# Attention loads and writes in half-size pieces, at most two under way: a linear-attention and expert kernel on one core

## The chip, the cores and the metric

The kernel runs on one core of one Trainium2 chip. The metric is device time in microseconds (us), as the median of several runs; a profiled execution of the same kernel gives the span and the trace that the views below are taken from. Engines are named as in the profile: PE (TensorE matmuls), PEld (TensorE weight loads), DVE (VectorE), ACT (ScalarE), POOL (GpSimd), SP (SyncE, whose queue issues the transfers that this document is about).

## What is computed

Linear attention without a softmax, an RMS norm, and then a layer of eight experts with balanced assignment. All data are float32.

```
kv  = einsum('bhsd,bhse->bhde', k, v)          # B=8, H=8, S=576, D=64
out = einsum('bhsd,bhde->bhse', q, kv)
x   = out / sqrt(mean(out^2) + 1e-6) * g_norm  # then (B*S, H*D) = (4608, 512)
logits = x @ w_gate                            # 8 experts, 576 tokens each
# greedy: all (token, expert) pairs in falling order of logit; a token takes
# the expert if it has none yet and the expert has room
out[tokens of e] = relu(x[tokens of e] @ w1[e]) @ w2[e]     # 512 -> 1024 -> 512
```

## The kernel before

The program has three stages, one after the other: attention, the assignment of tokens to the first expert, and the experts (with the next expert's assignment beside the matmuls of the present one). The change lies in the attention stage alone.

**Attention.** The loop runs over the eight batches b. `load(name, b)` brings one of k, v, q of a batch into a tile of 128 partitions x 4 head pairs (`NP`) x 9 rows (`R`) x 64, that is 1152 KB, by one transfer from SP (L75). Each of the three names has two buffers, so batch b + 2 takes the buffer of batch b. The first six loads (batches 0 and 1) are issued at the start. `prepare(b)` is a generator of four steps: it multiplies k by v into `kv_ps` (L273, 144 matmuls in two halves, head pairs 0 and 1 and then 2 and 3), adds the halves on ACT and DVE (`odd` L278, `kv` L280), copies the result to `kvx` on POOL (L286), calls for k and v of b + 2, transposes q into `qt` (L301), computes the gate's weights seen through kv (L312, L320), and last calls for q of b + 2. `work(b)` makes the output tiles of batch b: `tiles()` runs, for each of 3 to 5 token tiles, 32 small matmuls (`o_ps`, L349), a square and a copy on ACT (`sq` L355, `o_sb` L356), a reduction on DVE (`ms` L357); then the norm's factor, the logits `lg` (L371), and a copy of the factor into `o_sb` on POOL (L374). While batch b is worked on, the steps of `prepare(b + 1)` are laid between its tiles.

**Writes.** Each `o_sb` (4 or 5 token tiles of 128 x 576 numbers, 288 KB each; batch 7 makes two, of 3 and 2 token tiles) goes to `x_dram` by one transfer from SP (L375). The transfers are put on a list, `writes`, and issued in order at the end of a batch while the list holds `LAG = 5` or more; after batch 7 all are issued. `o_sb` has `LAG + 1 = 6` buffers, so batch 6 writes into batch 0's buffer and must find its write landed.

**Order.** In this stage PE, DVE, ACT and SP are under `manual_schedule`: their instructions run in the order in which the program makes them. So the queue of SP holds, in this order, the loads k0 v0 q0 k1 v1 q1 k2 v2 q2 ... q7, then nine writes, then the loads of the first expert's weights. Four small transfers (`g_col`, `gw`) are issued from ACT at the start.

**Assignment and experts.** `control(0)` finds thresholds by seven rounds of comparison on DVE (L242) and small matmuls (L440), then POOL gathers the rows of `x_dram` (L575); `layers(t)` runs the two matmuls of each expert (L639, L650).

The lines that tie the loads to the work are these:

```
    def prepare(b):                     # ... after the matmuls of kv(b)
        if b + 2 < B:
            load("k", b + 2)
            load("v", b + 2)
...                                     # ... after the transposes of q(b)
        if b + 2 < B:
            load("q", b + 2)
```

## Time and profile before

| | |
|---|---|
| median of 3 runs | 753.87 us (753.83 to 755.69) |
| profiled execution, its own time | 750.37 us |
| span in the trace | 748.4 us |
| PE busy | 640.3 us (86%) |
| attention stage, up to the last logits `lg` (L371) | 0 to 135.4 us |
| first assignment, up to the first row gather (L575) | 135.5 to 172.3 us |
| experts | 172.3 us to the end |
| PE idle in the attention stage put down to "issue", between 14 and 127 us | 25.3 us |
| loads of k, v and q | 24 of 1152 KB |
| writes of x_dram | 9: four of 1152 KB, three of 1440 KB, one of 864 KB, one of 576 KB |

The profiled execution is 3.50 us below the median of the runs; 1.97 us of its own time lie outside its span. "Issue" is idle time of an engine for which the trace shows no semaphore that it waited for. In the transfer views, "to landing" is the time from the issue on SP to the last of the transfer's completion counts.

### The profile page before, as it was taken

How to read it: one execution, taken by the hardware profiler on the slowest of the kernel's cores; microseconds unless marked ns; L12 is line 12 of the kernel's file. 1: busy time of each engine (PE TensorE's matmuls, PEld its weight loads, DVE VectorE, ACT ScalarE, POOL GpSimd, SP SyncE). 2: the span in 40 equal slices, each digit the busy share in tenths (PEclk: the TensorE clock that was granted, in tenths of full speed). 3: DMA queues.
4: the chain of work that ended last, by engine and by line, in shares of the span. 5: the costliest groups of instructions: out<-in, count | busy, mean ns of one | idle time of the engine just before them, and what ended most of it. 6: DMA issues, size and time to landing. Idle time of an engine off the chain costs nothing.

```text
span 748.4 us, 12187 instructions
## 1 busy us (share of the span) xinstructions
PE 640.3 (86%) x5001; PEld 405.7 (54%) x5001; DVE 352.9 (47%) x1253; ACT 161.6 (22%) x331; POOL 93.0 (12%) x113
## 2 busy tenths in 40 slices
PE   2787756113999999999999999999999999999994
PEld 2676645002764576457546744774476457547741
DVE  3455646785556365555645554656365642010000
ACT  0466446001110211021112112110211021122100
POOL 0101000002002300310031004001400322010011
PEclk9999998555999999999999999999999999999998
DMA  8988694108004500720090017004500638010001
GB/s 306 363 275 312 222 392 155 75 1 295 1 1 165 195 1 0 261 98 1 15 323 22 1 62 291 8 0 145 207 8 1 230 129 296 14 43 7 1 28 35
DMA packets 40838, 93.32 MB, mean 125 GB/s; under 512 B 2896, under 2 KB 2896, under 8 KB 40784
## 3 DMA queue, kind: packets, MB, share of 16 engines
q1 hardware_dynamic: 34192, 72.49, 27.2%
q0 software_dynamic: 5888, 20.06, 7.5%
q8 instruction: 39, 0.64, 0.3%
q10 hardware_dynamic: 704, 0.02, 0.1%
q14 instruction: 15, 0.12, 0.1%
HBM read 72.50 MB, written 20.05 MB: 124 GB/s over the span
## 4 chain that ended last, share of the span: by engine, by line
issue 62%; PE 17%; POOL 10%; DVE 7%; DMA 2%; ACT 1%; ACTq 0%; POOLq 0%; DVEq 0%
POOL out_dram L621 5%; POOL xg L575 5%; PE h_ps L639 5%; PE o_ps L349 3%; PE kv_ps L273 2%; PE qt_ps L301 2%; PE y_ps L650 2%; DMA gw<-in_moe_w_gate_dram 1%; DVE over L242 1%; DMA xg<-x_dram,ids 1%; PE n_ps L440 1%; ACT sq L355 1%; DVE ms L357 1%; DVE need L446 0%; PE w_ps L320 0%
## 5 line engine op out<-in xcount | busy, mean ns | idle before, releaser
L639 PE MATMUL h_ps<-xt,w_sb 128*128 128x288 f32 x1024 | 270.7, 415 | 0.0
L650 PE MATMUL y_ps<-w_sb,hid 128*128 128x512 f32 x512 | 227.2, 597 | 0.0
L639 PEld LDWEIGHTS h_ps<-xt,w_sb 128*128 128x128 f32 x1024 | 188.7, 191 | 51.9 <-issue 5.7
L650 PEld LDWEIGHTS y_ps<-w_sb,hid 128*128 128x128 f32 x512 | 94.8, 190 | 105.2 <-issue 104.3
L642 ACT ACTIVATE hid<-h_ps 128x288 f32<-128x288 f32 x128 | 52.5, 410 | 219.8 <-PE h_ps L639 219.8
L621 POOL DMA_INDIRECT out_dram<-y_sb,outs x40 | 41.1, 1026 | 452.5 <-ACT y_sb L653 401.6
L612 DVE TENSOR_TENSOR xs<-xg 128x512 f32<-128x512 f32 (+1 forms) x40 | 27.1, 690 | 90.9 <-DMA xg<-x_dram,ids 45.8
L242 DVE TENSOR_TENSOR over<-mx,cand 128x1152 bf16<-128x1152 f32 (+3 forms) x52 | 67.5, 1298 | 1.6
L653 ACT COPY y_sb<-y_ps 128x512 f32<-128x512 f32 x32 | 18.7, 585 | 209.2 <-PE y_ps L650 209.2
L663 DVE TENSOR_TENSOR y_sb<-y_ps,y_part 64x512 f32<-64x512 f32 x8 | 5.5, 683 | 95.4 <-ACT y_part L662 95.4
L575 POOL DMA_INDIRECT xg<-x_dram,ids x40 | 38.9, 972 | 73.2 <-DVE up L582 36.9
L349 PE MATMUL o_ps<-kvx,qt 64*64 64x72 f32 x1152 | 34.5, 247 | 15.3 <-issue 13.2
L349 PEld LDWEIGHTS o_ps<-kvx,qt 64*64 64x64 f32 x1152 | 27.5, 148 | 20.7 <-issue 16.6
L440 PEld LDWEIGHTS <-over 128*128 128x128 bf16 x441 | 18.1, 97 | 38.1 <-DVE over L242 22.9
L616 PE MATMUL t_ps<-ident,xs 128*128 128x128 f32 (+1 forms) x160 | 23.9, 284 | 17.1 <-DVE xs L612 13.7
L461 DVE SCALAR_TENSOR_TENSOR at<-row_f,k_ps,cand 128x33 f32<-128x33 f32 x98 | 21.4, 257 | 34.3 <-PE k_ps L456 34.3
L273 PE MATMUL kv_ps<-v_sb,k_sb 64*64 64x64 f32 x1152 | 27.2, 243 | 11.1 <-issue 11.1
L440 PE MATMUL n_ps<-best,over 128*128 128x32 bf16 x441 | 19.2, 178 | 20.4 <-DVE cand L434 12.5
L617 ACT ACTIVATE xt<-t_ps,g_col 128x512 f32<-128x512 f32 (+1 forms) x40 | 24.4, 646 | 52.5 <-PE t_ps L616 52.4
L446 DVE TENSOR_TENSOR need<-goal,n_ps 32x8 f32<-32x8 f32 x49 | 7.5, 154 | 57.0 <-PE n_ps L440 57.0
L357 DVE TENSOR_REDUCE ms<-sq 128x8 f32<-128x512 f32 x36 | 24.3, 681 | 19.5 <-ACT sq L355 19.4
L616 PEld LDWEIGHTS t_ps<-ident,xs 128*128 128x128 f32 (+1 forms) x160 | 18.0, 149 | 26.6 <-issue 16.4
(162 smaller groups left out, 472.6 us busy)
## 6 DMA issues: line engine op xcount, KB each, us to landing
w_sb<-in_moe_w_dram SPq DMA_DIRECT2D x16, 1024.0 KB, 6.1
w_sb<-in_moe_w_dram SPq DMA_DIRECT2D x8, 2048.0 KB, 16.1
k_sb<-in_k_dram SPq DMA_DIRECT2D x8, 1152.0 KB, 6.6
v_sb<-in_v_dram SPq DMA_DIRECT2D x8, 1152.0 KB, 9.4
q_sb<-in_q_dram SPq DMA_DIRECT2D x8, 1152.0 KB, 7.4
x_dram<-o_sb SPq DMA_DIRECT2D x4, 1152.0 KB, 13.0
x_dram<-o_sb SPq DMA_DIRECT2D x3, 1440.0 KB, 13.9
x_dram<-o_sb SPq DMA_DIRECT2D x1, 864.0 KB, 3.7
```

The costliest lines, as they stand in the source:

```text
L242: nc.vector.tensor_tensor(over[:, c0:c1], mx[:, c0:c1].rearrange("p (c o) -> p c o", o=1).to_broadcast([P, c1 - c0, NCAND]), cand[:, 1:NCA ...
L273: nc.tensor.matmul(kv_ps[cs, l, r * D:(r + 1) * D], lhsT=k_sb[ls, r, j, :], rhs=v_sb[ls, r, j, :], start=(j < 2), stop=(j >= R - 2))
L349: nc.tensor.matmul(o_ps[n * HP:(n + 1) * HP, rp, (2 * r2 + l) * W:(2 * r2 + l + 1) * W], lhsT=turned_q[bn][ks, block // 2, l * HP:(l + 1) ...
L357: nc.vector.reduce_sum(out=ms[:, t * H:(t + 1) * H], in_=sq, axis=AXX)
L440: nc.tensor.matmul(n_ps, lhsT=over[:, c:c + G].rearrange("p c n -> p (c n)"), rhs=best[:, c:c + G].rearrange("p c e -> p (c e)"), start=(c ...
L575: nc.gpsimd.indirect_dma_start(out=xg[0:nr].rearrange("p h w -> p (h w)"), out_offset=None, in_=x_dram, in_offset=bass.IndirectOffsetOnAxi ...
L612: nc.vector.tensor_tensor(xs[0:nr].rearrange("p (h d) -> p h d", h=H), xg[0:nr, :, 0:D], xg[0:nr, :, D:D + 1].to_broadcast([nr, H, D]), op ...
L616: nc.tensor.transpose(t_ps[:, d, 0:nr], xs[0:nr, d * P:(d + 1) * P], ident[0:nr, 0:nr])
L621: put = nc.gpsimd.indirect_dma_start(out=out, out_offset=bass.IndirectOffsetOnAxis(ap=ids_of[t][0:nr, n:n + 1], axis=0), in_=y_sb[0:nr, :] ...
L639: nc.tensor.matmul(h_ps, lhsT=w1[:, 2 * (d % 2) + d // 2, f * P:(f + 1) * P], rhs=xt[:, d, cs], start=(d == 0), stop=(d == DC - 1))
L642: nc.scalar.activation(hid[:, f, cs], h_ps, ACT.Relu)
L650: nc.tensor.matmul(y_ps, lhsT=hid[:, f, a:a + nr], rhs=w2[:, f, :], start=(f == 0), stop=(f == FC - 1))
```

## The change

Each load becomes two transfers of two head pairs (576 KB). Each write becomes transfers of two token tiles (576 KB), with a last one of a single token tile (288 KB) where the count is odd. All of them go through `paced()`, which keeps a list of the transfers in order and gives each one a dependence on the transfer two places ahead of it: SP issues it only when that one has landed. The list of writes is emptied down to fewer than ten entries at the end of a batch instead of five. `o_sb` keeps its six buffers and the loads their two.

```diff
     loaded = {}
+    AHEAD = 2
+    issued = []
+
+    def paced(dma):
+
+        if len(issued) >= AHEAD:
+            tc.add_manual_dep(dma.ins, issued[-AHEAD].name,
+                              mybir.DependencyInfo(mybir.DependencyClass.Sync, mybir.DependencyReason.DATA),
+                              reason="paced loads")
+        issued.append(dma.ins)
 
     def load(name, b):
 
         src = {"k": k, "v": v, "q": q}[name]
         t = att.tile([P, NP, R, D], FT, name=f"{name}_sb", tag=name, bufs=2)
-        nc.sync.dma_start(
-            t.rearrange("p r j d -> p r (j d)"),
-            src[b].rearrange("h s d -> (h s) d").rearrange("(r p j) d -> p r (j d)", r=NP, j=R))
+        rows = src[b].rearrange("h s d -> (h s) d").rearrange("(r p j) d -> p r (j d)", r=NP, j=R)
+        for r in range(0, NP, NP // 2):
+            rs = slice(r, r + NP // 2)
+            paced(nc.sync.dma_start(t[:, rs].rearrange("p r j d -> p r (j d)"), rows[:, rs]))
         loaded[name, b] = t
...
-        writes.append(lambda: nc.sync.dma_start(
-            x_dram[c0 * P:(c0 + T) * P, :].rearrange("(t p) f -> p t f", p=P), o_sb.rearrange("p t h w -> p t (h w)")))
+        for x in range(0, T, 2):
+            y = min(x + 2, T)
+            writes.append(lambda x=x, y=y: paced(nc.sync.dma_start(
+                x_dram[(c0 + x) * P:(c0 + y) * P, :].rearrange("(t p) f -> p t f", p=P),
+                o_sb[:, x:y].rearrange("p t h w -> p t (h w)"))))
...
-            while len(writes) >= LAG or b + 1 == B and writes:
+            while len(writes) >= 2 * LAG or b + 1 == B and writes:
                 writes.pop(0)()
```

In the built program SP's queue holds 48 load pieces and 20 write pieces. Counting the pieces a, b and c of a transfer, its order at the end of the stage is ... q6a q6b W0a k7a k7b v7a v7b q7a q7b W0b W1a W1b W1c W2a ..., where W0 is batch 0's `o_sb`. The matmuls of kv wait for the pieces of k and v half by half (head pairs 0 and 1 for `a`, 2 and 3 for `b`); the first ACT copy into a reused `o_sb` waits for all pieces of that buffer's last write.

## The prediction

> **What bounds the kernel now.** I read first the page's slices, then the chain of waits through the attention stage, then the idle times of PE there, then the transfers. The slices (18.7 us each) place the attention stage in the first seven:

> ```profile
> PE   2787756113999999999999999999999999999994
> ...
> DMA  8988694108004500720090017004500638010001
> ```

> PE is not full there (2 to 7 tenths), the DMA engines are 6 to 9 tenths busy; afterwards the first assignment (DVE) and then the experts (PE, 9 tenths) follow, and neither can start before the last logits. So a microsecond won in this stage should come off the end. The chain of waits through the stage runs over PE, and its largest pieces are of one kind:

> ```profile
> 26.41 3.60 issue
> ...
> 78.31 4.30 issue
> ...
> 94.78 5.34 issue
> ...
> 110.04 3.47 issue
> ```

> Each line is a start and a length. PE stands still in the middle of a run of matmuls whose inputs are already there. PE's own idle times between 14 and 127 us say the same; the columns are us in total, times, longest:

> ```profile
> PE o_ps L349 <- issue: 13.2, 7, 4.3
> PE kv_ps L273 <- issue: 11.1, 5, 5.3
> ```

> With two of 0.5 us that is 25.3 us, against 1.9 for the largest wait on another engine apart from the start. What ends them? I counted PE's instructions (weight loads and matmuls) in the trace. The halts stand before instructions 704, 1216, 1472, 1984, 2240, 2496, 2752, 3008, 3264, 3776, 4032, 4288, 4544: each 192 plus a multiple of 256. And the packet records of DMA queue 8 ("instruction") show 39 packets of 16,384 bytes for PE's 10,002 instructions, about 256 each. PE waits for its own program. The packet before a halt's end starts about 2.4 us ahead of it every time (80.24 for 82.62, 97.75 for 100.12): 1.1 us for the packet and 1.3 until PE runs. If PE asks for the next block when it enters a new one, the packet started 0.4 to 1.6 us later with nothing or little of k, v, q queued, and 3.3 to 5.0 us later with more than a transfer queued (69.7 to 73.5, 76.2 to 80.2, 92.7 to 97.75). The last is the window with the DMA engines full (us, then PE, PEld, DVE, ACT and POOL busy, clock, DMA share, GB/s):

> ```profile
> 91.60:108.70 17.10, 11.03 (x362) 9.60 (x357) 7.46 (x15) 8.11 (x17) 1.46 (x3) 0.90 1.04 389
> ```

> DVE and ACT are half idle there, so they aren't the bound. Nor are late loads: k and v of a batch are issued as soon as the buffer is free and land 5.4 and 9.2 us later at best, from batch 2 on 7 us and more before use.

> [...] Here a load alone needs 5.4 us for 1152 KB, of which 3.03 are bytes at 389 GB/s: 2.4 us fixed.

> **The change, part by part.**

> 1. *Shallower queue ahead of a fetch.* Before, up to 4 MB stood queued. After, at most two pieces (3.0 us of bytes), and since the second is mostly issued late, about one. I take 1.3 us as the mean start of a fetch, in place of the measured ones: each of the 13 halts shrinks by its own excess or vanishes. The four large ones give 2.2, 2.7, 3.7 and 2.0 us, the other nine 4 together (one gets 0.8 worse). So about 14.5 of the 25 us could go, if nothing else held PE: 12 us or so per batch instead of 14.1 (second half of kv1 at 30.0 to that of kv7 at 114.5: 84.5 us for six batches).

> 2. *Slower stream.* A 576 KB piece alone should need 2.4 + 1.5 = 3.9 us; SP reacts within 0.05 us (the load at 18.39 follows kv0's end at 18.35). With two in flight that is 2.0 us a piece, where the old stream needs 1.5. A fetch holds one DMA engine for 1.1 us[...]; a fetch each 5 us, with something absorbed in the gaps, adds about 0.17. I take 2.17 us. It isn't shown by this trace: a lower bound is 1.9 (fetches hidden in gaps, at the smallest fixed part), an upper one 2.5 (every fetch delays the stream whole). Working from the start with the slow first 8 us of the trace (about 260 GB/s): k0a lands at 5.5, k0b 7.7, v0a 9.8, v0b 11.8, and so on in steps of 2; v1b, the tenth piece, at 24. Then 36 pieces of loads and W0a lie ahead of v7b: 24 + 37 x 2.17 = 104.3 us. PE alone would be there at about 28 + 6 x 12 = 100. So the stream takes over as the bound, and kv7's second half stands at 104 instead of 114: 10 us gained so far. Batch by batch the waits on k and v are about 1 us.

> 3. *What is queued behind.* SP runs in order, so a waiting piece holds back every later one. W0b stands behind q7, and ACT's first copy into batch 6's `o_sb` waits for W0a and W0b. q7a is issued when v7a lands (102.1), lands 4.2 later (106.3), then W0b is issued and needs 2.9 us (the 576 KB write of the page): 109.2. Before, W0 landed at 102.1 and batch 6's first copy ran at 109.3, with 7 us to spare. The write's row among the transfers (KB each, us to landing), and the copy in ACT's timeline (start, us):

> ```profile
> x_dram<-o_sb SPq DMA_DIRECT2D x1, 576.0 KB, 2.9
> ```

> ```profile
> 109.29 0.63 ACT L356 COPY o_sb<-o_ps 128x576 f32<-128x576 f32 x1
> ```

> ACT must then do that copy, a square and a copy (1.6 us overlapped) before it reaches `odd` of kv7: 111 instead of 116.5. So 5.5 us remain of the 10. The later writes (W1c lands about 113.4, needed 9 us after W0b or more; W2b likewise) don't bind.

> 4. *At nothing:* 39 more issues on SP (0.37 to 0.5 us each, some 17 us) lie in SP's waits of over 100 us; the few more semaphore waits of PE likewise. The last writes end near 135, covered by the assignment, which keeps DVE busy to the gather at 172; without that cover they would cost a few us. g_col and gw on ACT's queue have less traffic beside them: 0 to 2 us at the start, which the stream to v1b takes back. The experts are unchanged.

> Sum: about 5 us off. Against the profiled execution's own 750.37 that is 745.4; the median of the runs stands 3.5 above it, so 753.87 - 5 = 748.9. A measurement of this kernel tells apart some 0.3%, 2.3 us.

> **The rivals.**

> - *Fetch-bound, with a quick stream.* If a piece needs 1.9 us, v7b is at 94, PE's own 100 us decides, and W0b is no later than before: 12 to 14 us off, 741. For it: the fixed part may overlap better. Against: 2.4 us were measured on lone loads.
> - *The stream is slower and ends the stage later: slower.* The mechanism is the same SP queue: landing, then issue, with k7, v7, q7, W0b in a row. Break-even is where v7b + 5 + 1.7 reaches 116.5, so v7b at 109.8 and a piece at 2.32 us. At 2.5 v7b is at 116.5, `odd` at 123, and the kernel 6.7 us slower: 760.6. For it: 1.1 us per fetch on one engine, and DMA share already 1.04 in one window; against: half-size pieces leave gaps that take fetches up.
> - *The fetch doesn't care for the queue's depth*, only for the transfer running. Then the 25 us stay in part, and the stream's pace with W0b eats the rest: no change, 751.6 to 756.
> - That the change doesn't do what it says is excluded by the built program: the waits on the piece two ahead, and by halves on PE, are there.

> **How the numbers follow.** Stream-bound with part of the gain kept (3 to 9 off) 0.46; quick stream 0.14; no change 0.18; slower 0.22. So faster 0.60, same 0.18, slower 0.22. The likeliest gives 748.9, its own range 745 to 751. For eight in ten I go from 741 (quick stream) to 758.5, between break-even and the slow stream's 760.6.

> **What would show it.** Right: idle "issue" of PE in the stage falls from 25 to 8 to 12 us, with no halt over 3; waits of PE on k or v appear, and SP's queue waits mostly on transfers; a load piece lands in about 4 us and pieces follow at 2.1 to 2.2; ACT's copy into batch 6's `o_sb` waits on a write; the last logits at about 130 instead of 135.4; from there to the end nothing moves. Wrong: if the halts stay above 20 us, step 1 falls; if PE waits on k or v for more than 20 us, step 2 was too low; if v7b lands before 98, it was too high; if batch 6's copy doesn't wait, step 3 falls.

## The result, and the profile after

The changed kernel takes 760.25 us (median of 4 runs, 757.8 to 760.86) against 754.38 us before (4 runs): a ratio of 1.0069, 95% interval 1.0042 to 1.0096. It is slower by some 5.9 us, where 5 us less were forecast. The profiled execution took 759.79 us with a span of 758.0, 9.6 us more than the span before; the execution shown of before was 4.0 us below this median of four runs, the one after 0.5, so the traces show the difference larger than the medians do.

The whole of it lies in the attention stage. The last logits end at 145.4 us instead of 135.4, the first row gather starts at 182.2 instead of 172.3, and from there to the end both kernels take 576 us. The page's slices after (18.95 us each) show the DMA engines at 7 to 8 tenths without a break through the stage, where before they went 8, 9, 8, 8, 6, 9, 4:

```profile
PE   4678766210999999999999999999999999999994
...
DMA  7888777806201800450072008002700548010001
```

PE's and ACT's idle times between 14 and 140 us after the change (us in total, times, longest):

```profile
PE kv_ps L284 <- DMA v_sb<-in_v_dram: 21.7, 8, 5.0
...
ACT o_sb L367 <- DMA x_dram<-o_sb: 13.3, 1, 13.3
...
PE o_ps L360 <- issue: 2.2, 3, 1.7
...
PE kv_ps L284 <- issue: 0.4, 2, 0.2
```

The 25.3 us of "issue" that PE stood idle before are 2.6 us now. In their place PE waits 21.7 us for v, in every batch from batch 1 on, and ACT waits 13.3 us once, for a write. The transfers after (KB each, us to landing):

```profile
k_sb<-in_k_dram SPq DMA_DIRECT2D x16, 576.0 KB, 4.7
v_sb<-in_v_dram SPq DMA_DIRECT2D x16, 576.0 KB, 4.7
q_sb<-in_q_dram SPq DMA_DIRECT2D x16, 576.0 KB, 5.1
x_dram<-o_sb SPq DMA_DIRECT2D x16, 576.0 KB, 3.2
```

And the chain of waits near the end of the stage (start, us, what):

```profile
105.38 4.17 DMA k_sb<-in_k_dram
109.57 5.54 DMA v_sb<-in_v_dram
115.18 3.81 DMA q_sb<-in_q_dram
119.05 5.04 DMA x_dram<-o_sb
124.16 0.65 ACT o_sb L367
```

This is every second piece in SP's queue, each issued when the one two places ahead had landed: k7a, v7a, q7a, W0b, and then the copy into batch 6's `o_sb` that needs batch 0's write out of the way. For these 19 us the chain runs over no engine; it is all transfers, one after the other.

The start moved too. PE's first matmul waits, through DVE, for the small transfer `gw`, and only then comes kv of batch 0. Before and after (start, us, instruction, idle time and what ended it; then DVE's wait for `gw`, us in total, times, longest):

```profile
13.64 0.59 PE L185 MATMUL g_ps<-g,ones_f 128*128 128x8 f32 x2 [13.64 <-DVE g L181]
...
DVE gw L103 <- DMA gw<-in_moe_w_gate_dram: 11.1, 1, 11.1
```

```profile
8.21 0.60 PE L196 MATMUL g_ps<-g,ones_f 128*128 128x8 f32 x2 [8.21 <-DVE g L192]
...
DVE gw L114 <- DMA gw<-in_moe_w_gate_dram: 5.6, 1, 5.6
```

With less queued beside it `gw` lands 4.8 us after its issue instead of 9.5 (medians of its two transfers), and PE starts 5.4 us earlier. In the changed kernel nothing of that is left by the second half of kv1 (26.3 us, before 25.7), since v1's second piece lands only at 26.0. In some of the runs below it is kept.

### The profile page after: what moved, and what is told of

The parts are those of the page before. It is cut to its first block, busy times and chain, and to the rows that moved or that the text cites. A ratio compares the mean times of both kernels' runs of the same rounds, so it can differ in the third digit from the quotient of the medians.

```text
span 758.0 us, 12248 instructions
## 1 busy us (share of the span) xinstructions
PE 652.5 (86%) x5001; PEld 416.9 (55%) x5001; DVE 352.6 (47%) x1253; ACT 161.6 (21%) x331; POOL 92.6 (12%) x113
## 4 chain that ended last, share of the span: by engine, by line
issue 57%; DMA 15%; PE 11%; POOL 10%; DVE 5%; ACT 0%; POOLq 0%; SPq 0%; DVEq 0%; ACTq 0%
DMA k_sb<-in_k_dram 5%; POOL out_dram L635 5%; DMA v_sb<-in_v_dram 5%; POOL xg L589 5%; PE h_ps L653 5%; DMA q_sb<-in_q_dram 3%; PE y_ps L664 2%; PE kv_ps L284 2%; DVE over L253 1%; PE o_ps L360 1%; DMA xg<-x_dram,ids 1%; DMA w_sb<-in_moe_w_dram 1%; DMA x_dram<-o_sb 1%; PE qt_ps L312 1%; PE n_ps L454 1%
## 5 line engine op out<-in xcount | busy, mean ns | idle before, releaser
L667 ACT COPY y_sb<-y_ps 128x512 f32<-128x512 f32 x32 | 18.7, 585 | 209.2 <-PE y_ps L664 209.2
L284 PE MATMUL kv_ps<-v_sb,k_sb 64*64 64x64 f32 x1152 | 34.8, 291 | 22.1 <-DMA v_sb<-in_v_dram 21.7
L284 PEld LDWEIGHTS kv_ps<-v_sb,k_sb 64*64 64x64 f32 x1152 | 32.3, 195 | 23.7 <-issue 15.8
L630 PE MATMUL t_ps<-ident,xs 128*128 128x128 f32 (+1 forms) x160 | 23.9, 284 | 16.5 <-DVE xs L626 12.8
## 6 DMA issues: line engine op xcount, KB each, us to landing
k_sb<-in_k_dram SPq DMA_DIRECT2D x16, 576.0 KB, 4.7
v_sb<-in_v_dram SPq DMA_DIRECT2D x16, 576.0 KB, 4.7
q_sb<-in_q_dram SPq DMA_DIRECT2D x16, 576.0 KB, 5.1
x_dram<-o_sb SPq DMA_DIRECT2D x16, 576.0 KB, 3.2
```

The source lines that it names most:

```text
L284: nc.tensor.matmul(kv_ps[cs, l, r * D:(r + 1) * D], lhsT=k_sb[ls, r, j, :], rhs=v_sb[ls, r, j, :], start=(j < 2), stop=(j >= R - 2))
```

## The experiments

**Theory 1**: the gain at the instruction fetch is real, and is spent again because a piece needs 4.7 to 5 us from issue to landing, so that two in flight make 2.45 us a piece; k and v come late, and W0b, behind q7, comes later still. **Rivals**: the halving itself costs; the pacing of the writes costs; or the halts of PE have nothing to do with the loads.

Four quantities are read from each trace. *Pace*: time from the issue of v1's last piece to that of v7's last, over the pieces between, for 576 KB. *Fetch*: from the moment PE enters a block of 256 instructions to the start of the packet that is taken to bring the next one, mean and longest (blocks and packets are paired in order; up to 140 us of the change one packet starts between each two block boundaries). *Halts*: time from the start of one matmul to the start of the next at the block boundaries, where it is over 0.35 us, 14 to 128 us. It takes in the matmul itself, some 0.25 us each time, and, close to a boundary, up to 1.0 us of a wait for another engine; so before has 29.5 us here and 25.3 us of idle time. *Logits*: where the last logits end. The pace of before is set by its buffers, not by its transfers: up to 140 us SP waits 69.6 us for PE's work on k, v and q, and 0.2 us for a load of theirs. Each ratio is to the runs of before on the same chip.

| kernel | ratio (95%) | median us | pace us | fetch us | halts us | logits us |
|---|---|---|---|---|---|---|
| before | 1 | 754.4 | (2.18) | 2.65, 5.2 | 29.5 | 135.4 |
| the change | 1.0069 (1.0042 to 1.0096) | 760.3 | 2.47 | 1.66, 2.7 | 4.5 | 145.4 |
| halves_free | 1.0048 (1.0024 to 1.0072) | 757.3 | 2.05 | 2.89, 4.7 | 31.9 | 140.1 |
| ahead3 | 0.9913 (0.9878 to 0.9949) | 747.9 | 1.99 | 2.51, 4.1 | 23.9 | 132.1 |
| ahead4 | 0.9967 (0.9942 to 0.9992) | 752.0 | 2.00 | 2.60, 5.6 | 28.2 | 135.1 |
| whole_ahead2 | 0.9959 (0.9935 to 0.9984) | 750.6 | 2.03 | 3.03, 4.6 | 31.8 | 140.4 |
| write0_early | 1.0000 (0.998 to 1.002) | 753.9 | 2.45 | 1.59, 3.0 | 5.0 | 139.7 |
| whole_writes_free | 1.0074 (1.0049 to 1.0098) | 759.4 | 2.44 | 1.79, 3.9 | 5.7 | 142.5 |
| few_loads | 0.9728 (0.9695 to 0.9761) | 734.2 | none | 1.42, 4.5 | 13.0 | 120.0 |
| ahead1 | one run | 832.8 | 3.86 | not read | 0.3 | 214.6 |
| quarter4 | 0.9829 (0.9794 to 0.9864) | 742.2 | 2.20 | 1.49, 2.6 | 14.1 | 127.0 |
| quarter6 | 0.9854 (0.9812 to 0.9895) | 745.0 | 1.88 | 2.24, 4.1 | 26.0 | 130.0 |

A profiled execution lies up to 5 us off its kernel's median (whole_ahead2: 755.7 against 750.6), so the last column is read for order of size alone, and the fetches and halts are those of one execution each.

**halves_free: the pieces without the pacing**

```diff
-    AHEAD = 2
+    AHEAD = 1000
```

> Pieces as in the change, pacing taken out (AHEAD = 1000, so no piece waits for another one but through its buffer). Theory 1 (the pacing costs: a piece needs 4.7 to 5 us from issue to landing, two in flight make 2.45 us a piece): the stream runs at about 1.5 us a piece again, PE's wait on k and v and ACT's wait on the write of batch 0 go, PE's halts for instructions come back to 15 to 25 us, 750 to 756 us in all. Rival (the halving itself costs, more transfers and more restarts): about 760 us, k and v still late.

Measured: 757.3 us, 1.3 us past the upper end of what theory 1 allowed and 3 us short of the rival. k, v and the write of batch 0 are in time again, no wait of PE or ACT on a transfer is left in the list, and the halts are all back (31.9 us, more than the 15 to 25 expected). So late k and v come from the pacing. But the halving is not free: 0.48% slower than before, with as many halts and fetches that start 0.24 us later on average. Why halves alone cost that stays open.

**ahead3 and ahead4: three and four pieces in flight**

```diff
-    AHEAD = 2
+    AHEAD = 3
```

> Three pieces in flight instead of two, all else as in the change. Theory 1: 4.9 / 3 = 1.6 us a piece, so v7's second half lands at about 26 + 37 x 1.65 = 87 us, before PE needs it; halts for instructions stay below 12 us; logits end near 125 to 130, 743 to 748 us. Rival (halving costs, or the transfers slow each other): 757 us or more.

> Four pieces in flight. Theory 1: the stream is no bound (1.5 us a piece), the queue ahead of an instruction fetch is about twice as deep as in the change, halts 8 to 18 us: 745 to 751 us, so not better than three. Rival (halving costs): 757 us or more.

Measured: 747.9 and 752.0 us. With three the kernel is faster than before by 0.87%: the sign of the change turns on one piece more in flight. Nobody waits for k or v. The pace is 2.0 us, not 1.6. With three, SP still waits mostly for landings (49 us between 20 and 95 us, against 11 for buffers), and a landing takes 5.4 to 5.8 us where 4.9 had been assumed; with four it waits more for buffers (34 against 22). The halts, though, are 23.9 us, twice what was expected. PE's idle times of ahead3:

```profile
PE o_ps L360 <- issue: 12.9, 7, 3.7
PE kv_ps L284 <- issue: 5.8, 3, 2.5
```

The longest wait of a fetch grows with the depth: 2.7 us with two pieces, 4.1 with three, 5.6 with four, 5.2 before. That is step 1 of the prediction, by degrees. The small halts of the change (4.5 us) are probably in part a cover, since PE stood waiting for v while the block came.

Shorter halts are not all of ahead3's gain. Its PE starts kv of batch 0 at 11.9 us instead of 14.2, and at the second half of kv1 it is 2.3 us ahead (23.4 us instead of 25.7); at the last logits it is 3.3 us ahead. With four pieces the start is no earlier (14.1 us).

**whole_ahead2: the pacing without the halving**

```diff
-        for r in range(0, NP, NP // 2):
-            rs = slice(r, r + NP // 2)
+        for r in range(0, NP, NP):
+            rs = slice(r, r + NP)
...
-        for x in range(0, T, 2):
-            y = min(x + 2, T)
+        for x in range(0, T, T):
+            y = min(x + T, T)
...
-            while len(writes) >= 2 * LAG or b + 1 == B and writes:
+            while len(writes) >= LAG or b + 1 == B and writes:
```

> Pacing as in the change (two places ahead) with transfers of the whole size, loads 1152 KB and writes of a whole o_sb. Theory 1: bytes in flight are as with four halves; about 3.1 to 3.3 us a load, 26 us + 18.5 x 3.2 = 85 for v7: the stream is no bound, halts 8 to 20 us, 745 to 752 us. Rival (it is the wait on a landing as such, whatever the size): 757 us or more.

Measured: 750.6 us, inside what theory 1 said, and not slow as the rival had it; its halts (31.8 us) are above the 8 to 20 expected. A wait on a landing did no harm here with 2.3 MB under way (ratio 0.9959), and no help to the fetch shows (3.03 us on average, before 2.65). The four halves of ahead4 come out about the same.

**write0_early: W0b ahead of k7**

```diff
-            while len(writes) >= 2 * LAG or b + 1 == B and writes:
+            while len(writes) >= 2 * LAG - 1 or b + 1 == B and writes:
```

> The change with one thing moved: the list of writes is emptied down to fewer than nine entries, so both pieces of batch 0's write stand ahead of k7 in SP's queue, not one. Theory 1 (the last step of the delay is W0b behind q7, which ACT's copy waits for): ACT's 13 us wait goes, the stream to v7 gets one piece longer (2.45 us, v7's second half lands near 119), so the matmuls of kv7 set the end: some 4 us faster than the change, 755 to 757 us. Rival (the wait on the write only covers the lateness of k and v, which is the whole cost): no gain, 760 to 763 us.

Measured: 753.9 us, no different from before (1.0000), some 5 to 6 us faster than the change and 1 us better than theory 1 allowed; the rival is out. The waits on transfers of PE and ACT in it:

```profile
PE kv_ps L284 <- DMA v_sb<-in_v_dram: 22.2, 7, 5.2
ACT o_sb L367 <- DMA x_dram<-o_sb: 1.6, 2, 1.2
```

ACT's 13.3 us have become 1.6, and PE waits for v as long as in the change. So the two delays come apart: k and v late by 2.45 us a piece cost what the shorter fetches and the earlier start gained (balance nil), and the place of W0b in the queue is the net loss.

**whole_writes_free: only the loads paced**

```diff
-        for x in range(0, T, 2):
-            y = min(x + 2, T)
-            writes.append(lambda x=x, y=y: paced(nc.sync.dma_start(
+        for x in range(0, T, T):
+            y = min(x + T, T)
+            writes.append(lambda x=x, y=y: (nc.sync.dma_start(
...
-            while len(writes) >= 2 * LAG or b + 1 == B and writes:
+            while len(writes) >= LAG or b + 1 == B and writes:
```

> The loads as in the change (half pieces, two in flight), the writes as before (whole, waiting on no other transfer). Theory 1: no piece of a write stands ahead of k7 (2.45 us off) and batch 0's write goes out as soon as q7 is issued, not landed: 755 to 758 us; k and v stay late, at 2.4 us a piece. Rival (pacing the writes is what costs): 750 us or less.

Measured: 759.4 us, as slow as the change and 1.4 us past theory 1's upper end; the rival is out. Undoing the pacing of the writes helps nothing: batch 0's write still stands behind q7 in SP's queue, and q7 comes at the pace of the loads. ACT waits 11.4 us for it.

**few_loads: PE without the traffic** (batches 2 to 7 use the tiles of batches 0 and 1; the loads for them are left out, so it computes something else and stands for its time alone)

```diff
+        if b >= 2:
+            loaded[name, b] = kept[name, b % 2]
+            return
         t = att.tile([P, NP, R, D], FT, name=f"{name}_sb", tag=name, bufs=2)
+        kept[name, b] = t
```

> The kernel before without the loads of k, v and q for batches 2 to 7; those batches use the tiles of batches 0 and 1. What is left is PE's work with hardly any traffic beside it up to the writes. If PE's halts come from instruction fetches that wait behind the loads: fetches start 0.5 to 2 us after PE enters a block, halts fall from 29.5 us to under 12, logits end 12 to 18 us sooner, 736 to 742 us. Rival (the halts are PE's own and need no traffic): halts above 20 us, 750 us or more.

Measured: 734.2 us, 2.7% less than before and 2 us better than expected; logits 15.4 us sooner, halts 13.0 us, one above the expected limit. The windows from 24 to 108 us, of before and then of this kernel (us; PE, PEld, DVE, ACT, POOL busy; clock, DMA share, GB/s):

```profile
24.00:108.00 84.00, 60.38 (x1953) 52.14 (x1951) 43.72 (x88) 44.59 (x89) 8.52 (x17) 0.92 0.85 304
```

```profile
24.00:108.00 84.00, 69.33 (x2266) 60.33 (x2263) 51.74 (x109) 52.07 (x104) 10.00 (x20) 0.89 0.27 98
```

In the same 84 us PE gets through 2266 matmuls instead of 1953. The loads cost 15 us of the stage, and the halts shrink by about as much (29.5 to 13.0). The traffic that is left is the writes, and the three longest fetches (4.5, 3.4 and 3.2 us) each come within 3 us after a write was issued. The 15 us are about what shorter halts could win at most; the earlier start is not in it, for PE starts kv of batch 0 at 14.0 us here too.

**ahead1: what one piece needs alone**

```diff
-    AHEAD = 2
+    AHEAD = 1
```

> The change with one piece in flight. It measures what one 576 KB piece needs alone, the term that the prediction put at 3.9 us (2.4 fixed and 1.5 of bytes). If that was right, pieces follow every 4.0 us and the logits end near 205 us; if a restart of the DMA engines after a pause costs more for each piece, 4.4 us or more a piece and the end near 225 us. PE's halts nearly vanish either way.

Measured: one piece lands in 3.8 us, the next follows after 3.86:

```profile
k_sb<-in_k_dram SPq DMA_DIRECT2D x16, 576.0 KB, 3.8
```

So the lone time of the prediction (3.9) was right as a sum, and the rival reading, that a restart makes each piece dearer, falls for lone pieces. The logits end at 214.6 us, 10 us later than the 205 that went with it. The miss in the pace is in what two pieces do to each other: 4.7 to 5.1 instead of 3.8.

The parts of the sum were not those of the prediction. By the packet records, the first packet of a lone piece starts 1.0 us after the issue, its packets run over 2.4 us, and the last count comes 0.4 us after them. The prediction had 2.4 us fixed and 1.5 of bytes, its author's estimate from 5.4 us to landing and 389 GB/s; here 1.4 us lie outside the packets, and the packets take 2.4.

**quarter4 and quarter6: the bytes in flight of two and of three halves, cut finer** (AHEAD = 4 or 6, pieces of one head pair or one token tile)

```diff
-    AHEAD = 2
+    AHEAD = 4
...
-        for r in range(0, NP, NP // 2):
-            rs = slice(r, r + NP // 2)
+        for r in range(0, NP, NP // 4):
+            rs = slice(r, r + NP // 4)
...
-        for x in range(0, T, 2):
-            y = min(x + 2, T)
+        for x in range(0, T, 1):
+            y = min(x + 1, T)
...
-            while len(writes) >= 2 * LAG or b + 1 == B and writes:
+            while len(writes) >= 3 * LAG or b + 1 == B and writes:
```

> Quarter pieces (288 KB, one head pair or one token tile), four in flight: the same 1152 KB in flight as in the change, cut finer; all four pieces of batch 0's write stand ahead of k7, as the two do in the run write0_early (753.9 us). Theory 1 (with few pieces in flight the pace is set by the time from issue to landing, which a smaller piece shortens): some 3.4 to 3.8 us a piece, 1.7 to 1.9 us per 576 KB instead of 2.45; k and v hardly late, fetches still start within 3 us: 742 to 748 us. Rival (the bytes in flight set the pace, or each restart of the DMA engines costs): 2.3 us or more per 576 KB and 752 us or more.

> Quarter pieces, six in flight: the 1728 KB in flight of the run ahead3 (747.9 us), cut finer. Theory 1: the stream is no bound, the fetches wait as long as in ahead3 (longest about 4 us), halts 18 to 24 us: 745 to 750 us, no better than quarter4. Rival (what counts for the fetch is the size of a single transfer, not the bytes in flight): halts below 12 us and 744 us or less.

Measured: 742.2 and 745.0 us; quarter4 beats both kernels, by 1.7% against before. Its fetches start about like those of the change (mean 1.49 us, longest 2.6), while its stream needs 2.20 us per 576 KB instead of 2.47. The time that theory 1 named for quarter4 holds, its pace of 1.7 to 1.9 does not. Of two halves the version to set beside quarter4 is write0_early, which has the whole of batch 0's write ahead of k7 too: 1.0000 against 0.983. PE's waits in quarter4:

```profile
PE kv_ps L284 <- DMA v_sb<-in_v_dram: 10.7, 7, 4.8
PE kv_ps L284 <- issue: 5.8, 3, 2.5
PE o_ps L360 <- issue: 4.8, 5, 2.1
```

Half the wait for v is gone. But a piece of half the bytes still needs about the same time to landing with three others under way (k 4.6 us, v 3.9, q 4.7): the rival's view, that bytes in flight over a nearly fixed time make the pace, is closer there (2.20 beside its 2.3), though its total of 752 us is out. Why the finer cut gains the 0.25 us was not tested. quarter6 has the halts of ahead3's depth (26.0 us, above the 18 to 24 expected) and its longest fetch (4.1 us in both), so here the size of a single transfer was not what a fetch waited for.

Much of both gains comes from the start: kv of batch 0 begins at 9.0 and 9.1 us, and at the second half of kv1 quarter4 is 4.0 us ahead of before and quarter6 4.9 (21.7 and 20.8 us instead of 25.7). At the last logits they are 8.4 and 5.4 us ahead. So about half of quarter4's gain in the trace, and nearly all of quarter6's, is there before most of the fetches; no run separates the start from the rest.

**shift64: 64 more instructions on PE ahead of everything**

```diff
-    nc.tensor.matmul(g2_ps, lhsT=ones_f, rhs=g2, start=True, stop=True)
+    for _ in range(17):
+        nc.tensor.matmul(g2_ps, lhsT=ones_f, rhs=g2, start=True, stop=True)
```

> The kernel before with 16 copies of one small matmul (L185) at the start of PE's stream, 64 instructions more in the trace (four per float32 matmul), 1 to 3 us. If PE halts for blocks of 256 instructions, the halts stay at the numbers 192 + 256 n counted from the start and so come 64 instructions earlier in the work. Rival (the halts belong to places in the work, such as a batch's second half of kv): they stand at 256 n.

The halts stand before instructions 704, 1216, 1472, 1984, 2240, 2752, 3264, 3520, 4032, 4544 and 4800, all 192 + 256 n, though other matmuls stand there now. They follow the count. The 17 matmuls took 7.4 us, much more than the 1 to 3 expected, so its 765.0 us say nothing more.

## Why the prediction was wrong

**What bounds the kernel: right.** PE's halts are instruction blocks that come late because of the loads: in few_loads the halts are 13.0 us instead of 29.5, and in shift64 they stay at 192 + 256 n. Two corrections: the numbers of the halts counted PE's semaphore instructions too, not weight loads and matmuls alone; and two of the thirteen (3008 and 3776) are of 0.2 us.

**Step 1, a shallower queue brings the blocks sooner: right.** 1.3 us was forecast for the start of a fetch, 1.66 measured (2.65 before), the longest 2.7 instead of 5.2. A reading beside it was off: the second half of kv1 begins at 25.7 us, and 30.0 is where PE goes on after a halt inside it, so a batch took 14.7 us and not 14.1.

**Step 2 failed, at the price of a piece.** It took half the lone time, 3.9 / 2, plus an estimated 0.17 for fetches: 2.17 us. Measured: 2.47. The lone time was right (3.8), so the halving of it is the term. In the trace of the change the 24 load pieces with no whole fetch in their time took 4.7 us to landing, the other 24 took 5.1 (medians). That is 0.2 us of landing on average, or 0.1 us of the pace, for the fetches, so they weren't priced too low: two pieces under way lengthen each other by some 0.9 us even without a fetch, which the step left out.

Why they do is argued, not shown. Halving 3.9 assumes that one piece's 1.5 us of bytes are under way while the other's 2.4 us run. With packets over 2.4 us of a lone piece, and not 1.5, two pieces in turn come to 2.4 us each, close to 2.47. But ahead3 has a pace of 1.99, so with three under way such stretches overlap in part. No run varies this alone.

PE's 21.7 us for v passed the 20 us that the prediction gave as the sign that this step was too low. Over 37 pieces the 0.30 us make 11. v1b landed at 26.0 instead of 24, v7b at 116.7 instead of 104.3, and from the second half of kv1 to that of kv7 it took 92 us (26.3 to 118.2) where before it took 88 (25.7 to 114.0): the stream ate the whole gain of step 1 and of the earlier start. In the medians that balance is write0_early's ratio of 1.

**Step 3, W0b behind q7: right in mechanism, too small.** It was to be ACT's wait at 109.2; it ended at 124.2. Of the 15 us, 12.4 are v7's lateness from step 2. Most of the rest is the write, 5.0 us instead of 2.9: the row it was read from was a write alone on the queue, and here a load piece ran beside it. write0_early prices the place in the queue at 5 to 6 us.

**The nothings of step 4: right but for the start.** PE's start came 5.4 us earlier, not 0 to 2; that the stream to v1b takes it back was right for this kernel. The experts take 576 us in both; the late writes (the last is issued at 150.5 us) end well before the gather at 182.

**The rivals.** The slow stream was named with its point of decision, 2.32 us a piece, and its price, 760.6 us at 2.5; the chip gave 2.47 and 760.25. That the totals agree so well is in part luck: in the trace `odd` of kv7 came at 125.9 us, not at the 123 that went with 760.6. This rival had 0.22. The mistake was in weighing: a bound of 2.5 stood beside a value of 2.17 for a term that no row of before showed, and 0.1 us of it is worth 3.7 us of the result, so the sign was open. The range ended at 758.5, short of the case that came.

## What to carry to other kernels

Holding transfers back to let small urgent ones through worked here, for PE's instruction blocks (a fetch starts after 1.66 us instead of 2.65) and for the small transfer that PE's start waits for (4.8 us to landing instead of 9.5). But with two half pieces under way the pace came to about half the time from issue to landing (2.47 us, of 4.7 to 5.1), and that time grew with each piece added: 3.8 us alone, 4.7 to 5.1 with two, 5.4 to 5.8 with three. Measure it with the depth that is meant, not with a lone piece. Try one step deeper, or the same bytes in finer pieces, before giving up: here two halves lose 0.7% (nothing with the write moved), three win 0.9%, four quarters win 1.7%. Where a queue runs in the program's order, as SP's does here, look for what stands behind the paced transfers: W0b, a write that frees a buffer, was issued at 119.05 us, just after q7a had landed (118.99), and this made the whole net loss of 5 to 6 us.
